# Quarter sums of the expert weights: loaded quarters against units already in SBUF

## The chip, the cores and the metric

The kernel runs on one core of a Trainium2 chip. The metric is the device time of one execution in microseconds (us). Engines are called as in the profile: PE (TensorE), PEld (its weight loads), DVE (VectorE), ACT (ScalarE), POOL (GpSimd) and SP (SyncE, which issues all of this kernel's DMAs).

## The reference

Attention over 8 batches of 12 heads, 448 positions, 64 elements a head, with a mix of the heads before and after the softmax; then an expert layer over all 3584 positions:

```
scores = einsum('bhij,hg->bgij', q @ k^T / 8, w_pre)
attn   = softmax(scores) ; attn = einsum('bhij,hg->bgij', attn, w_post)
x      = (attn @ v), heads side by side               # 3584 x 768
out    = ((x @ w1) * (x @ w2)) @ w3 @ w_out           # 768 -> 1024 -> 1024 -> 768
```

All in float32. The weights w1, w2, w3 and w_out come as float64.

## The kernel before

**The main loop.** `run` goes through N = 360 steps, 45 for each batch; a step handles 10 of the 448 rows of all 12 heads (120 partitions). The order of the work is written out by hand; each engine works through its own queue in that order. In step n stand, one behind the other: the fetch of the score rows of step n + 4 (L194), then whatever was put off to "later" (stores, loads of weights; `do_later`), splits of q and k for a later batch, the softmax of step n (DVE's reduce L218, ACT's exponent L221), the scaled mix weights of step n - 1 (L230 to L233), the split of the rows of step n + 2 into a rounded and a rest part (DVE L201, POOL L202), products q k^T of the next batch (L174, L175, left through ACT's copy L179 "st"), the work on expert weights that this text is about, half of the step's share of expert matmuls, the mix after the softmax for step n - 2 (`post`, L241, left through ACT's copy L247 "mt" out of bank 4), the products with v (L272), the other half of the expert matmuls, and the mix before the softmax for step n + 1 (L209 to L211). At the end `do_ends` issues the copies out of PSUM.

**Precision.** Products are made of float32 numbers split into a rounded part (type float32r) and a rest: three matmuls for each product (`PAIRS`). So a 128 x 128 block of a weight is kept as "hi" and "lo" side by side.

**The experts, batches 0 and 1 (`ONE` = 2).** `expert_atoms` makes the plain product, as background work of so many matmuls a step (`shares` spreads them evenly). The weights come in "units": for w1 and w2 one column block f of 128 with all six row blocks (768 KB, 18 matmuls), for the product w3 w_out, which is made beforehand, half a column block d (four row blocks, 512 KB, 12 matmuls). `next_unit` takes the next one, three buffers in pool "wp", two loads ahead. Batch 0's units of w1 and w2 are converted from float64 in SBUF and stored; all others are loaded (L354). Batch 0's first layer (288 matmuls) goes over steps 53 to 106, its output layer (144) and all of batch 1 (432) over steps 107 to 188, some 7 a step.

**The experts, batches 2 to 7.** From step 190 (`PAIR`) two batches at a time are multiplied by a scheme of seven products for 2 x 2 blocks in place of eight. Each weight is a 2 x 2 of quarters x11, x12, x21, x22, and four of the seven products need sums of quarters: number 7 is x11 - x21, number 5 is x21 + x22, number 6 is number 5 - x11, number 3 is x12 - number 6. These are stored split as "s_d" (L439) before step 190 and loaded by the pair stage.

**How the sums are made.** `combining` (L407 to L470) is a generator that is taken one piece further in each step once the conversion of units is over (L886). It has 12 sets: four for w1, four for w2, four for the third weight. A set takes 7 steps: two quarters are loaded (L423, tile "l", in the "s" buffers), in the next step DVE adds hi and lo of both (L430) and takes the first difference (L442); ACT and POOL split the result into an "s" tile (L436, L437), which is stored a step later (L439); then the other quarters are loaded in the same way, one a step. The "s" buffers are three, shared by the loads and the splits.

```
l11, l21 = (load(*sets[0], 0, i) for i in range(2))
yield
for i, (w, f) in enumerate(sets):
    x11, x21 = whole("x", f"x11{n}", l11), whole("x", f"x21{n}", l21)
    ...
    sum(s3, x11, x21, ALU.subtract)
    yield
```

Of the kernel before, what the change touches and what calls it, by code (L numbers as in the profile page):

```python
# [16 lines left out]
IB = 10  # L17
# [24 lines left out]
class Kernel:  # L42
# [219 lines left out]
    def av(self, b, a, g):  # L262
        nc, cols = self.nc, self.cols(a)
        W = cols.stop - cols.start
        if g % 3 == 0:
            self.i_psa = self.next_bank() if self.xq else 5
            self.psa = self.bank(self.i_psa, f"psa{b}_{a}_{g}")[:, :3 * GB * IB].rearrange("p (g i) -> p g i", g=3)
        v, mt = self.vs.pop((b, a, g)), self.mt[b, a]
        for j in range(NJ):
            for s in range(2):  # L270
                rows = slice(s * D, (s + 1) * D)
                nc.tensor.matmul(self.psa[rows, g % 3, :W], v[:, j, rows], mt[:, j, 2 * g + s, :W],  # L272
                                 start=(j == 0), stop=(j == NJ - 1))
        if g % 3 == 2 and b >= ONE:
            q, dst = self.psa[:, :, :W], self.x_d[b][g // 3][:, :, cols]
            x = self.staging(f"xd{b}_{a}_{g}")[:, :, :W]

            def leave():
                nc.scalar.copy(x, q)
                self.later.append(store)  # L280

            def store():
                nc.sync.dma_start(dst, x)
                self.x_made[b] += 1

            self.ends.append((self.i_psa, leave))
        elif g % 3 == 2:
            if b not in self.xs:
                pool = self.xp[b % 2]
                self.xs[b] = [pool.tile([128, K1, S], F32R, tag=f"x{t}", name=f"x{t}{b}") for t in "hl"]  # L290
            h, l = (x[:, g - 2:g + 1, cols] for x in self.xs[b])
            q = self.psa[:, :, :W]
            self.ends.append((5, lambda: nc.scalar.copy(h, q)))
            self.soon.append((5, lambda: nc.vector.tensor_tensor(l, q, h.bitcast(F32), op=ALU.subtract)))
        self.later.append(self.load_v)

    def staging(self, name):

        self.n_staging += 1
        if self.xq:  # L300
            return self.xq.tile([128, 3, GB * IB], F32, tag="x", name=name)
        t = self.xp[0].tile([128, K1, S], F32R, tag="xh" if self.n_staging % 2 else "xl", name=name)
        return t.bitcast(F32).rearrange("p k s -> p (k s)")[:, :3 * GB * IB].rearrange("p (k s) -> p k s", k=3)
# [44 lines left out]
    def units(self):  # L348
        return [u for b in range(ONE) for u in
                [(w, f, 0) for f in range(KF) for w in range(2)] + [(3, d, q) for d in range(K1) for q in range(2)]]  # L350

    def load_unit(self):
        t, src = self.unit_from(f"wu{self.n_loaded}", *self.unit_list[self.n_loaded])
        self.nc.sync.dma_start(t.bitcast(F32), src)  # L354
        self.loaded.append(t)
        self.n_loaded += 1
        self.n_asked -= 1

    def unit_of_one(self, name, w, f, q):
        t = self.wp.tile([128, K1, 2, 128], F32R, tag="w", name=name)  # L360
        if w < 2:
            return t, self.w_d[w][f]
        h = KF // 2
        return t[:, :h], self.w34_d[f][:, q * h:(q + 1) * h]

    def unit_of_pair(self, name, w, f, m):
        h, c = (K1 // 2, KF // 2) if w < 2 else (KF // 2, K1 // 2)
        t = self.wp.tile([128, KF // 2, 2, 128], F32R, tag="w", name=name)[:, :h]
        src = self.w_d[w] if w < 2 else self.w34_d
        if m in (1, 2, 4):  # L370
            return t, src[f + c * (m == 4)][:, h * (m > 1):h * (1 + (m > 1))]
        return t, self.s_d[w][m][f]
# [34 lines left out]
    def combining(self):  # L407

        nc, h = self.nc, K1 // 2
        sets = [(w, f) for w, f in [(0, 0), (1, 0), (0, 1), (1, 1), (0, 2), (1, 2), (0, 3), (1, 3)]]  # L410
        sets += [(2, f) for f in range(KF // 2)]

        def tile(name):
            return self.cs.tile([128, CW, 2], I32, tag="s", name=name, bufs=3).rearrange(
                "p n b -> p (n b)").bitcast(F32).rearrange("p (k t c) -> p k t c", k=h, t=2)

        def load(w, f, kh, fh):
            t = tile(f"l{w}_{f}_{kh}{fh}")
            if w < 2:
                src = self.w_d[w][f + fh * KF // 2][:, kh * h:(kh + 1) * h]  # L420
            else:
                src = self.w34_d[fh * h:(fh + 1) * h, :, f + kh * KF // 2].rearrange("d p t c -> p d t c")
            nc.sync.dma_start(t, src)  # L423
            return t

        def whole(tag, name, t):
            x = self.cs.tile([128, CW], F32, tag=tag, name=name, **({"bufs": 1} if tag == "m" else {}))
            x = x.rearrange("p (k c) -> p k c", k=h)
            if t is not None:
                nc.vector.tensor_tensor(x, t[:, :, 0], t[:, :, 1], op=ALU.add)  # L430
            return x

        def split(w, f, m, x):
            t = tile(f"s{w}_{f}_{m}")
            hi, lo = (t[:, :, i].bitcast(F32R) for i in range(2))
            nc.scalar.copy(hi, x)  # L436
            nc.gpsimd.tensor_tensor(lo, x, hi.bitcast(F32), op=ALU.subtract)  # L437
            dst = self.s_d[w][m][f] if w < 2 else self.s_d[w][m][:, :, f].rearrange("d p t c -> p d t c")
            self.later.append(lambda: nc.sync.dma_start(dst, t))  # L439

        def sum(out, x, y, op):
            nc.vector.tensor_tensor(out, x, y, op=op)  # L442

        l11, l21 = (load(*sets[0], 0, i) for i in range(2))
        yield
        for i, (w, f) in enumerate(sets):
            n = f"{w}_{f}"
            x11, x21 = whole("x", f"x11{n}", l11), whole("x", f"x21{n}", l21)
            s3 = whole("m", f"s3{n}", None)
            sum(s3, x11, x21, ALU.subtract)  # L450
            yield
            split(w, f, 7, s3)
            l22 = load(w, f, 1, 1)
            yield
            l12 = load(w, f, 1, 0)
            yield
            x22 = whole("m", f"x22{n}", l22)
            sum(x21, x21, x22, ALU.add)
            sum(x11, x21, x11, ALU.subtract)
            yield  # L460
            split(w, f, 5, x21)
            split(w, f, 6, x11)
            x12 = whole("m", f"x12{n}", l12)
            sum(x12, x12, x11, ALU.subtract)
            yield
            split(w, f, 3, x12)
            yield
            if i + 1 < len(sets):
                l11, l21 = (load(*sets[i + 1], 0, j) for j in range(2))
            yield  # L470
# [5 lines left out]
    def expert_atoms(self, b):  # L476
        nc, xs, hs = self.nc, self.xs.pop(b), []
        for f in range(KF):
            for i in range(2):
                w = self.next_unit()  # L480
                p = self.bank(6 + i, f"eg{b}_{f}_{i}")[:, :S]
# [18 lines left out]
            hs.append((h, l))  # L500
        self.do_ends()
        self.do_soon()
        for d in range(K1):
            p = self.bank(6 + d % 2, f"eo{b}_{d}")[:, :S]
            for k in range(KF):
                if k % (KF // 2) == 0:
                    w = self.next_unit()
                for t, (x, y) in enumerate(PAIRS):
# [6 lines left out]
            def leave(d=d, o=o, p=p, dst=dst):  # L515
                (nc.scalar.copy if d % 2 else nc.vector.tensor_copy)(o, p)
                self.later.append(lambda: nc.sync.dma_start(dst, o))

            self.ends.append((6 + d % 2, leave))
# [171 lines left out]
    def run(self):  # L691
# [5 lines left out]
        self.xq, self.n_staging = None, 0  # L697
# [5 lines left out]
        self.s_d = [{m: dp.tile([c, 128, k, 2, 128], F32, name=f"s{i}_{m}_d") for m in (3, 5, 6, 7)}  # L703
# [108 lines left out]
        self.unit_from, self.w_made, combining = self.unit_of_one, 2 * KF, self.combining()  # L812
        unit_pieces = self.converting(self.unit_jobs())
        nq, n_pieces = 0, -2
        for n in range(N + 6):
            if n == GB + 1:
                self.close("qp")
                self.xp = [self.pool("xp0", 1)]
            if n == SWITCH:
# [11 lines left out]
                background, total, done = self.experts(), (E_1 + E_2) * ONE, 0  # L831
            if n == PAIR:
                assert done == total and unit_pieces is None
# [4 lines left out]
                for _ in combining or ():  # L838
                    assert False
                self.close("sp", "hp", "xp1", "wp", "cs", "xp0")  # L840
                self.xq = self.pool("xq", 2)
# [44 lines left out]
            elif unit_pieces is None and combining and next(combining, self) is self:  # L886
                combining = None
# [78 lines left out]
```

## Time and profile before

| | us |
|---|---|
| median of 3 runs | 1742.28 (1741.29 to 1751.07) |
| profiled execution | 1747.12 |
| its span, first to last instruction | 1745.3 |
| mean granted PE clock | 0.967 |

| engine | busy us | share of the span |
|---|---|---|
| PE | 1616.8 | 93% |
| PEld | 1445.2 | 83% |
| DVE | 1110.5 | 64% |
| ACT | 929.9 | 53% |
| POOL | 1067.7 | 61% |

465 MB are moved in all, 266 GB/s over the span. Line numbers (L430) are those of the kernel before. In views of groups, "x48" is the number of instructions, followed by busy us, mean ns of one, and the idle time of the engine just before them with what ended it. In views of waits "A <- B: 82.6, 29, 8.4" says that A's engine sat idle 82.6 us in 29 places, at most 8.4 us, until B was done. In views of stretches each row begins with the stretch in us from the span's start; step 104 begins at 468 us, step 190 at 870 us.

### The profile page before, as it was taken

To read this page: it belongs to the slowest core of one execution; us is meant where nothing else is said; L and a number is where in the kernel's file an instruction comes from. 1 tells how busy PE (TensorE), PEld (TensorE's weight loads), DVE (VectorE), ACT (ScalarE), POOL (GpSimd) and SP (SyncE) were. 2 spreads that over 40 slices of the span, in tenths; PEclk is the share of its full clock that TensorE was granted. 3 is DMA by queue.
4 is the path that set the end of the run, shared out by engine and by line. 5 is a ranking of instruction groups with operands and counts; after the bars stand their busy time and mean duration, and the time that the engine had idled before them with its cause. 6 is when DMAs were issued, how large, how long until landed. Compare 5 with 4: busy or idle time off the path is not lost. (4 is left out here: it accounts for less than half of the span.)

```text
span 1745.3 us, 31764 instructions
## 1 busy us (share of the span) xinstructions
PE 1616.8 (93%) x10548; PEld 1445.2 (83%) x10548; DVE 1110.5 (64%) x2594; ACT 929.9 (53%) x2164; POOL 1067.7 (61%) x926
## 2 busy tenths in 40 slices
PE   4899998999989989888979999999999999999999
PEld 1479997887878878777869989989999899899988
DVE  4958657777656457556637557676665676844663
ACT  3867656767655455444545565556565444443222
POOL 2656545666655556455647677787676656756674
PEclk6999999999989999989989999999999999999999
DMA  7989778989889989988987898878987966669875
GB/s 257 289 261 286 242 214 259 290 282 305 265 275 326 339 289 313 327 261 274 309 271 231 267 298 241 264 243 259 334 271 243 265 188 196 196 212 321 279 233 183
DMA packets 242689, 464.97 MB, mean 266 GB/s; under 512 B 21854, under 2 KB 170590, under 8 KB 242526
## 3 DMA queue, kind: packets, MB, share of 16 engines
q1 hardware_dynamic: 242526, 462.95, 84.2%
q8 instruction: 84, 1.38, 0.3%
q14 instruction: 79, 0.65, 0.1%
HBM read 328.78 MB, written 134.09 MB: 265 GB/s over the span
## 5 line engine op out<-in xcount | busy, mean ns | idle before, releaser
L202 POOL TENSOR_TENSOR rl<-r,rh 120x448 fp32r<-120x448 f32 x360 | 430.3, 1196 | 487.3 <-DVE rh L201 136.7
L221 ACT ACTIVATE e<-psm,mn 120x448 f32<-120x448 f32 x360 | 228.6, 635 | 493.6 <-DVE sa L230 402.3
L241 PEld LDWEIGHTS pso<-w,e 120*112 120x112 f32 (+1 forms) x2880 | 354.9, 182 | 109.3 <-ACT mt L247 96.2
L218 DVE TENSOR_REDUCE mn<-psm 120x1 f32<-120x448 f32 x360 | 223.4, 621 | 344.7 <-PE psm L211 344.2
L241 PE MATMUL pso<-w,e 120*112 120x120 f32 (+1 forms) x2880 | 372.2, 274 | 70.0 <-ACT mt L247 69.7
L652 PE MATMUL e<-eh,wu 128*128 128x448 f32 x1008 | 305.7, 373 | 0.6 <-DVE c L606 0.5
L247 ACT COPY mt<-pso 112x480 f32<-112x480 f32 x360 | 206.2, 573 | 41.9 <-PE pso L241 41.0
L652 PEld LDWEIGHTS e<-eh,wu 128*128 128x128 f32 x1008 | 188.1, 189 | 15.7 <-DVE c L606 1.5
L201 DVE CAST rh<-r 120x448 fp32r<-120x448 f32 x360 | 184.6, 513 | 15.1 <-DMA r<-raw_d 14.6
L652 PE MATMUL e<-el,wu 128*128 128x448 f32 x504 | 187.7, 373 | 3.0 <-POOL el L591 3.0
L179 ACT COPY st<-psq 112x448 f32<-112x448 f32 x336 | 173.9, 528 | 28.9 <-DMA raw_d<-st 28.8
L233 DVE TENSOR_SCALAR w<-wpo,ri 120x120 f32<-120x120 f32 x360 | 161.8, 449 | 12.6
L209 PE MATMUL psm<-rh,wph 120*120 120x448 f32 x360 | 142.2, 395 | 20.0 <-DVE rh L201 20.0
L272 PE MATMUL psa<-mt,v 112*64 112x150 f32 (+1 forms) x2304 | 160.0, 296 | 0.0
L272 PEld LDWEIGHTS psa<-mt,v 112*64 112x64 f32 x2304 | 146.3, 139 | 6.6 <-issue 1.1
L484 PE MATMUL eg<-xh,wu 128*128 128x448 f32 x384 | 132.3, 395 | 7.3 <-ACT wu L113 4.5
L211 PE MATMUL psm<-rl,wph 120*120 120x448 f32 x360 | 134.9, 375 | 1.6 <-POOL rl L202 1.5
L164 POOL TENSOR_TENSOR ql<-kq,qh 128x448 fp32r<-128x448 f32 x84 | 97.5, 1160 | 61.1 <-ACT qh L162 60.8
L210 PE MATMUL psm<-rh,wpl 120*120 120x448 f32 x360 | 134.2, 373 | 0.0
L606 DVE TENSOR_TENSOR c<-c,e 128x448 f32<-128x448 f32 x168 | 100.9, 614 | 51.9 <-PE e L652 47.4
L174 PE MATMUL psq<-kk,qh 128*112 128x448 f32 x336 | 126.7, 377 | 6.7 <-ACT st L179 6.5
L175 PE MATMUL psq<-kk,ql 128*112 128x448 f32 x336 | 124.8, 371 | 0.0
(113 smaller groups left out, 2893.0 us busy)
## 6 DMA issues: line engine op xcount, KB each, us to landing
r<-raw_d SPq DMA_DIRECT2D x352, 210.0 KB, 4.0
raw_d<-st SPq DMA_DIRECT2D x168, 392.0 KB, 4.6
wu<-s_d SPq DMA_DIRECT2D x96, 384.0 KB, 4.2
v<-v SPq DMA_DIRECT2D x144, 224.0 KB, 4.8
kq<-kq SPq DMA_DIRECT2D x42, 672.0 KB, 7.4
wu<-w_d SPq DMA_DIRECT2D x72, 384.0 KB, 5.5
wu<-w_d SPq DMA_DIRECT2D x51, 512.0 KB, 6.1
l<-w_d SPq DMA_DIRECT2D x48, 384.0 KB, 7.3
```

Of the source, the lines that this page charges most:

```text
L179: copy(st[:, c % 2], p)
L201: nc.vector.tensor_copy(rh[:K], r[:K])
L202: nc.gpsimd.tensor_tensor(rl[:K], r[:K], rh[:K].bitcast(F32), op=ALU.subtract)
L209: nc.tensor.matmul(p[:K, :S], self.wph[:K, :K], rh[:K], start=True, stop=False)
L211: nc.tensor.matmul(p[:K, :S], self.wph[:K, :K], rl[:K], start=False, stop=True)
L218: nc.vector.tensor_reduce(mn[:K], p[:K, :S], axis=AX.X, op=ALU.min)
L221: nc.scalar.activation(e[:K], p[:K, :S], AF.Exp, bias=mn[:K], scale=-1.0, accum_out=sm[:K])
L233: nc.vector.tensor_scalar_mul(w2[:K, :, :w], wv[:K, :, :w], ri[:K])
L241: nc.tensor.matmul(p[:, j, :, :w], e[:K, j * JT:(j + 1) * JT], w2[:K, :, :w], start=True, stop=True)
L247: self.ends.append((4, lambda: copy(dst, p[:, :, :, :w])))
L272: nc.tensor.matmul(self.psa[rows, g % 3, :W], v[:, j, rows], mt[:, j, 2 * g + s, :W], start=(j == 0), stop=(j == NJ - 1))
L652: nc.tensor.matmul(p, w[:, k, x], ops[m, k][y], start=(k == 0 and t == 0), stop=(k == nk - 1 and t == 2))
```

## The change

`combining` and its 48 loads of quarters are gone. Where the experts take a unit whose quarters are wanted (the output layer of batch 0, the first layer of batch 1), `seen` is called: one step later DVE adds hi and lo straight from the unit's tile into a tile "y"; when both row halves of a block are there, `sums` takes the four sums in place over the next two steps, and the splits follow four to six steps after the unit was taken. `order` takes the blocks in the order 0, 4, 1, 5, ... (0, 3, 1, 4, ... for the output layer), so that the two blocks of a set are near each other. "y" has four buffers in a new pool "cb", made at step 107 together with the pool "xq" of the staged x, where the pool of batch 0's x is closed. A sum is stored with all hi ahead of all lo; for the third weight hi and lo are two stores, and lo is written over the sum in "y".

```
 def units(self):
     return [u for b in range(ONE) for u in
-            [(w, f, 0) for f in range(KF) for w in range(2)] + [(3, d, q) for d in range(K1) for q in range(2)]]
+            [(w, f, 0) for f in self.order(KF, b == 1) for w in range(2)] +
+            [(3, d, q) for d in self.order(K1, b == 0) for q in range(2)]]
...
+def seen(self, w, f, q, t):
+    c, k = (KF // 2, K1 // 2) if w < 2 else (K1 // 2, KF // 2)
+    halves = range(2) if w < 2 else (q,)
+    def whole():
+        if halves[0] == 0:
+            self.ys[w, f] = self.cb.tile([128, 2, 512], F32, tag="y", name=f"y{w}_{f}")
+        y = self.ys[w, f]
+        for i in halves:
+            u = t[:, i * k:(i + 1) * k] if w < 2 else t
+            u = u.bitcast(F32)
+            x = y[:, i, :k * 128].rearrange("p (k c) -> p k c", k=k)
+            self.nc.vector.tensor_tensor(x, u[:, :, 0], u[:, :, 1], op=ALU.add)
+    self.at(1, whole)
+    if f >= c and halves[-1] == 1:
+        self.sums(w, f - c, k)
+
+def sums(self, w, f, k):
+    ...
+    def first():
+        a, b = self.ys.pop((w, f)), self.ys.pop((w, f + c))
+        x.update({11: a[:, 0, :n], 12: a[:, 1, :n], 21: b[:, 0, :n], 22: b[:, 1, :n]})
+        nc.vector.tensor_tensor(x[11], x[11], x[21], op=ALU.subtract)
+        nc.vector.tensor_tensor(x[21], x[21], x[22], op=ALU.add)
+    def second():
+        nc.vector.tensor_tensor(x[22], x[22], x[11], op=ALU.subtract)
+        nc.vector.tensor_tensor(x[12], x[12], x[22], op=ALU.subtract)
+    def split(m, q):
+        s = self.cs.tile([128, CW, 2], I32, tag="s", name=f"s{w}_{f}_{m}", bufs=3)
+        ...
+        hi, lo = s[:, :n], s[:, n:2 * n] if w < 2 else x[q]
+        nc.scalar.copy(hi.bitcast(F32R), x[q])
+        nc.gpsimd.tensor_tensor(lo.bitcast(F32R), x[q], hi, op=ALU.subtract)
+        if w < 2:
+            self.later.append(lambda: nc.sync.dma_start(self.s_d[w][m][f], s))
         else:
+            self.later.append(lambda: nc.sync.dma_start(dst[:, 0], hi))
+            self.later.append(lambda: nc.sync.dma_start(dst[:, 1], lo))
+    self.at(2, first)
+    self.at(3, second)
+    for delay, m, q in ((4, 7, 11), (4, 5, 21), (5, 6, 22), (6, 3, 12)):
+        self.at(delay, lambda m=m, q=q: split(m, q))
...
 (expert_atoms)
+        for f in self.order(KF, b == 1):
             for i in range(2):
                 w = self.next_unit()
+                if b == 1:
+                    self.seen(i, f, 0, w)
...
+        if n == LATE:
+            self.close("xp0")
+            self.xq, self.cb = self.pool("xq", 2), self.pool("cb", 4)
...
-        elif unit_pieces is None and combining and next(combining, self) is self:
-            combining = None
+        self.do_timed()
```

More of the change, by code (lines that the diff above doesn't have):

```diff
@@ L265, in av @@
         if g % 3 == 0:
-            self.i_psa = self.next_bank() if self.xq else 5
+            self.i_psa = self.next_bank() if self.pairs else 5
             self.psa = self.bank(self.i_psa, f"psa{b}_{a}_{g}")[:, :3 * GB * IB].rearrange("p (g i) -> p g i", g=3)
@@ L275, in av @@
             q, dst = self.psa[:, :, :W], self.x_d[b][g // 3][:, :, cols]
-            x = self.staging(f"xd{b}_{a}_{g}")[:, :, :W]
+            x = self.xq.tile([128, 3, GB * IB], F32, tag="x", name=f"xd{b}_{a}_{g}")[:, :, :W]
             def leave():
@@ L295, in av @@
         self.later.append(self.load_v)
[L297 to L303, printed above, removed]
     def fold_jobs(self):
@@ L349, in units, with order @@
         return [u for b in range(ONE) for u in
-                [(w, f, 0) for f in range(KF) for w in range(2)] + [(3, d, q) for d in range(K1) for q in range(2)]]
+                [(w, f, 0) for f in self.order(KF, b == 1) for w in range(2)] +
+                [(3, d, q) for d in self.order(K1, b == 0) for q in range(2)]]
+    def order(self, n, summed):
+        return [i + j for i in range(n // 2) for j in (0, n // 2)] if summed else range(n)
     def load_unit(self):
-        t, src = self.unit_from(f"wu{self.n_loaded}", *self.unit_list[self.n_loaded])
+        t, view, src = self.unit_from(f"wu{self.n_loaded}", *self.unit_list[self.n_loaded])
         self.nc.sync.dma_start(t.bitcast(F32), src)
-        self.loaded.append(t)
+        self.loaded.append(view)
         self.n_loaded += 1
@@ L359, in unit_of_one @@
     def unit_of_one(self, name, w, f, q):
-        t = self.wp.tile([128, K1, 2, 128], F32R, tag="w", name=name)
+        t, h = self.wp.tile([128, K1, 2, 128], F32R, tag="w", name=name), KF // 2
         if w < 2:
-            return t, self.w_d[w][f]
-        h = KF // 2
-        return t[:, :h], self.w34_d[f][:, q * h:(q + 1) * h]
+            return t, t, self.w_d[w][f]
+        return t[:, :h], t[:, :h], self.w34_d[f][:, q * h:(q + 1) * h]
     def unit_of_pair(self, name, w, f, m):
         h, c = (K1 // 2, KF // 2) if w < 2 else (KF // 2, K1 // 2)
-        t = self.wp.tile([128, KF // 2, 2, 128], F32R, tag="w", name=name)[:, :h]
+        t = self.wp.tile([128, KF // 2 * 256], F32R, tag="w", name=name)[:, :h * 256]
         src = self.w_d[w] if w < 2 else self.w34_d
         if m in (1, 2, 4):
-            return t, src[f + c * (m == 4)][:, h * (m > 1):h * (1 + (m > 1))]
-        return t, self.s_d[w][m][f]
+            t = t.rearrange("p (k t c) -> p k t c", k=h, t=2)
+            return t, t, src[f + c * (m == 4)][:, h * (m > 1):h * (1 + (m > 1))]
+        return t, t.rearrange("p (t k c) -> p k t c", k=h, t=2), self.s_d[w][m][f]
     def unit_jobs(self):
@@ L403, in next_unit, with at @@
         return t
[L407 to L418, printed above, removed]
+    def at(self, delay, f):
+        self.timed.append((self.step + delay, f))
@@ new lines, in do_timed @@
+    def do_timed(self):
+        now = [f for n, f in self.timed if n <= self.step]
+        self.timed = [x for x in self.timed if x[0] > self.step]
+        for f in now:
+            f()
+    def seen(self, w, f, q, t):
[13 more added lines that the diff above has]
+            self.sums(w, f - c, k)
@@ new lines, in sums @@
+    def sums(self, w, f, k):
+        nc, c, n = self.nc, (KF // 2 if w < 2 else K1 // 2), k * 128
+        x = {}
+        def first():
[8 more added lines that the diff above has]
+            s = self.cs.tile([128, CW, 2], I32, tag="s", name=f"s{w}_{f}_{m}", bufs=3)
+            s = s.rearrange("p n b -> p (n b)").bitcast(F32)
+            dst = self.s_d[w][m][f].rearrange("p (t n) -> p t n", t=2)
+            hi, lo = s[:, :n], s[:, n:2 * n] if w < 2 else x[q]
+            nc.scalar.copy(hi.bitcast(F32R), x[q])
+            nc.gpsimd.tensor_tensor(lo.bitcast(F32R), x[q], hi, op=ALU.subtract)
@@ L419, in load @@
             if w < 2:
-                src = self.w_d[w][f + fh * KF // 2][:, kh * h:(kh + 1) * h]
+                self.later.append(lambda: nc.sync.dma_start(self.s_d[w][m][f], s))
             else:
[L422 to L470, printed above, removed]
+                self.later.append(lambda: nc.sync.dma_start(dst[:, 0], hi))
@@ L476, in expert_atoms @@
     def expert_atoms(self, b):
-        nc, xs, hs = self.nc, self.xs.pop(b), []
-        for f in range(KF):
+        nc, xs, hs = self.nc, self.xs.pop(b), {}
+        for f in self.order(KF, b == 1):
             for i in range(2):
                 w = self.next_unit()
+                if b == 1:
+                    self.seen(i, f, 0, w)
                 p = self.bank(6 + i, f"eg{b}_{f}_{i}")[:, :S]
@@ L499, in expert_atoms @@
             self.soon.append((None, parts))
-            hs.append((h, l))
+            hs[f] = h, l
         self.do_ends()
         self.do_soon()
-        for d in range(K1):
-            p = self.bank(6 + d % 2, f"eo{b}_{d}")[:, :S]
+        for n, d in enumerate(self.order(K1, b == 0)):
+            p = self.bank(6 + n % 2, f"eo{b}_{d}")[:, :S]
             for k in range(KF):
@@ L507, in expert_atoms @@
                     w = self.next_unit()
+                    if b == 0:
+                        self.seen(2, d, k // (KF // 2), w)
                 for t, (x, y) in enumerate(PAIRS):
@@ L513, in expert_atoms, with leave @@
             dst = self.out[d * 128:(d + 1) * 128, b * S:(b + 1) * S]
-            def leave(d=d, o=o, p=p, dst=dst):
-                (nc.scalar.copy if d % 2 else nc.vector.tensor_copy)(o, p)
+            def leave(n=n, o=o, p=p, dst=dst):
+                (nc.scalar.copy if n % 2 else nc.vector.tensor_copy)(o, p)
                 self.later.append(lambda: nc.sync.dma_start(dst, o))
-            self.ends.append((6 + d % 2, leave))
+            self.ends.append((6 + n % 2, leave))
     def pair_units(self):
@@ L696, in run @@
         self.slot, self.free, self.keep, self.x_made, self.n_groups = {}, list(range(NS)), [], [0] * B, 0
-        self.xq, self.n_staging = None, 0
+        self.timed, self.ys, self.pairs = [], {}, False
         dp = self.pool("dram", 1, space=DRAM)
@@ L702, in run @@
         self.x_d = [dp.tile([2, 128, K1 // 2, S], F32, name=f"x{b}_d") for b in range(B)]
-        self.s_d = [{m: dp.tile([c, 128, k, 2, 128], F32, name=f"s{i}_{m}_d") for m in (3, 5, 6, 7)}
+        self.s_d = [{m: dp.tile([c, 128, k * 256], F32, name=f"s{i}_{m}_d") for m in (3, 5, 6, 7)}
                     for i, (c, k) in enumerate(((KF // 2, K1 // 2), (KF // 2, K1 // 2), (K1 // 2, KF // 2)))]
@@ L811, in run @@
         self.unit_list, self.loaded, self.n_loaded, self.n_asked, self.w_ahead = self.units(), [], 0, 0, 2
[L812 removed]
+        self.unit_from, self.w_made = self.unit_of_one, 2 * KF
         unit_pieces = self.converting(self.unit_jobs())
@@ L815, in run @@
         for n in range(N + 6):
+            self.step = n
             if n == GB + 1:
@@ L831, in run @@
                 background, total, done = self.experts(), (E_1 + E_2) * ONE, 0
+            if n == LATE:
+                assert done >= E_1
+                self.close("xp0")
+                self.xq, self.cb = self.pool("xq", 2), self.pool("cb", 4)
             if n == PAIR:
-                assert done == total and unit_pieces is None
+                assert done == total and unit_pieces is None and not self.timed
                 next(background, None)
@@ L837, in run @@
                 self.do_later()
[L838 to L841, printed above, removed]
+                self.pairs = True
+                self.close("sp", "hp", "xp1", "wp", "cs", "cb")
                 self.wp = self.pool("wp", 5, side="right")
```

## The prediction

> **What bounds the kernel now.** I read the page first, then busy time by stage, then the waits of DVE and PE in the one stage that the change touches, then the instructions around one of those waits in order of time. A "step" is one turn of the main loop; each has one softmax reduce (L218), so counting L218 in a stretch counts its steps. The three long stretches below are most of batch 0's first layer (305.5 to 456.1), the stage in which the sums are made now (466 to 870) and a part of the pair stage (918.2 to 1290). Columns: length, busy us and instruction count of each engine (PE, PEld, DVE, ACT, POOL), granted clock, DMA share, GB/s.
>
> ```profile
> 305.50:456.10 150.60, 141.29 (x1013) 123.82 (x1013) 117.49 (x308) 106.22 (x251) 101.56 (x91) 1.00 0.92 288
> 466.00:870.00 404.00, 351.23 (x2312) 315.43 (x2310) 236.90 (x543) 202.81 (x484) 219.91 (x192) 0.93 0.93 301
> 918.20:1290.00 371.80, 368.48 (x2536) 338.35 (x2535) 249.50 (x571) 220.06 (x510) 267.06 (x226) 1.00 0.86 270
> 550.00:600.00 50.00, 45.79 (x312) 41.70 (x312) 28.96 (x66) 26.37 (x63) 27.53 (x25) 0.90 0.98 326
> 1600.00:1700.00 100.00, 99.25 (x489) 91.08 (x488) 63.47 (x83) 25.40 (x50) 70.45 (x59) 1.00 0.82 258
> ```
>
> The same three stretches for L218 alone (DVE's count is that of the steps), and for the experts' matmuls alone (PE and PEld; L484 in two stretches, then L509, then L652):
>
> ```profile
> 305.50:456.10 150.60, 24.77 (x40) 1.00 0.92 288
> 466.00:870.00 404.00, 53.35 (x87) 0.93 0.93 301
> 918.20:1290.00 371.80, 55.93 (x90) 1.00 0.86 270
> ```
>
> ```profile
> 305.50:456.10 150.60, 55.60 (x204) 35.66 (x204) 1.00 0.92 288
> 466.00:870.00 404.00, 83.31 (x310) 58.26 (x310) 0.93 0.93 301
> ```
>
> ```profile
> 466.00:870.00 404.00, 76.34 (x288) 53.31 (x288) 0.93 0.93 301
> ```
>
> ```profile
> 918.20:1290.00 371.80, 190.07 (x776) 139.84 (x776) 1.00 0.86 270
> ```
>
> In the pair stage PE idles 1% and a step takes 371.8 / 90 = 4.13 us with 776 / 90 = 8.6 expert matmuls; PE sets it. In the tail, where PE does nothing else, 489 of them take 100 us: 0.204 us each. The sums' stage has (310 + 288) / 86 = 6.95 expert matmuls a step (the 87th reduce only starts there), and PE's other work per step is that of the pair stage, so PE alone would need 4.13 - 1.67 x 0.204 = 3.79 us. It takes 404 / 86 = 4.70. So **78 us** (86 x 0.91) of this stage are not PE's work at full clock. They show as 53 us of idle PE and a clock of 0.93 instead of 1.00, some 28 us. By the same working batch 0's first layer needs 3.41 us and takes 3.77: 0.35 us a step too long at a DMA share of 0.92, with the clock at 1.00.
>
> What ends the idle times (who <- releaser: us, times, longest), DVE's and PE's in 466 to 870, then DVE's and PE's in 305.5 to 456.1:
>
> ```profile
> DVE x L430 <- DMA l<-w_d: 82.6, 29, 8.4
> DVE mn L218 <- PE psm L211: 75.0, 39, 6.1
> ```
>
> ```profile
> PE pso L241 <- ACT mt L247: 44.2, 14, 6.5
> PE psq L174 <- ACT st L179: 3.8, 1, 3.8
> PE eg L484 <- DVE em L491: 2.4, 1, 2.4
> PE eo L509 <- DMA wu<-w_d: 2.2, 1, 2.2
> ```
>
> ```profile
> DVE mn L218 <- PE psm L211: 24.7, 14, 3.1
> ```
>
> ```profile
> PE pso L241 <- ACT mt L247: 9.1, 13, 1.5
> ```
>
> DVE waits 82.6 us for the quarters that the sums load; in the stretch before it waits for PE and hardly else. One such wait in order of time:
>
> ```profile
> 505.59 2.72 SPq L423 DMA_DIRECT2D l<-w_d  x2
> ...
> 513.52 0.56 DVE L430 TENSOR_TENSOR x<-l 128x384 f32<-128x384 f32 x1 [5.79 <-DMA l<-w_d]
> ...
> 516.39 0.63 ACT L221 ACTIVATE e<-psm,mn 120x448 f32<-120x448 f32 x1 [7.54 <-DVE sa L230]
> ...
> 517.59 0.72 PE L174 MATMUL psq<-kk,qh 128*112 128x448 f32 x1 [3.83 <-ACT st L179]
> ...
> 522.09 0.37 PE L174 MATMUL psq<-kk,qh 128*112 128x448 f32 x1
> ```
>
> Two loads are issued at 505.6; DVE has stood at the first add for 5.8 us when it can run. The softmax reduce queued behind it is late, so ACT's exponent and, behind that in ACT's queue, the copies that free PE's banks; PE runs dry for 3.8 us, and its next matmul takes 0.72 us where the same one takes 0.37 us a step later. Twelve sets, each with such a wait, make the 78 us.
>
> The half rate after 3.8 us of idling is what the 0.93 is made of. The Trainium skill, TensorE: Matmul & The Clock Gate (Part 1), says that PE drops to half clock after an idle window of about 3.4 us and is back after as long a busy one; the 0.72 against 0.37 agrees. By that rule the clock's 28 us come back whole once no wait is that long; if the clock followed PE's mean load instead, half might stay away and the time below would be 14 us longer.
>
> **The change part by part.** *Removed: 48 loads* of 384 KB, and with them DVE's wait. Rows of 466 to 870: the DMA issues (count, KB each, median us to landing), and the sums' operations (busy, mean ns):
>
> ```profile
> l<-w_d SPq DMA_DIRECT2D x48, 384.0 KB, 7.3
> s_d<-s SPq DMA_DIRECT2D x48, 384.0 KB, 4.7
> ```
>
> ```profile
> L442 DVE TENSOR_TENSOR x<-x,x 128x384 f32<-128x384 f32 x36 | 40.1, 1114 | 1.2
> L437 POOL TENSOR_TENSOR s<-x,s 128x384 fp32r<-128x384 f32 x36 | 39.1, 1098 | 0.0
> L430 DVE TENSOR_TENSOR x<-l 128x384 f32<-128x384 f32 x48 | 30.6, 638 | 82.6 <-DMA l<-w_d 82.6
> L436 ACT CAST s<-x 128x384 fp32r<-128x384 f32 x36 | 17.5, 523 | 0.0
> ...
> L437 POOL TENSOR_TENSOR s<-s,s 128x384 fp32r<-128x384 f32 x12 | 12.0, 999 | 0.0
> L442 DVE TENSOR_TENSOR s<-x,x 128x384 f32<-128x384 f32 x12 | 6.7, 558 | 1.2
> L436 ACT CAST s<-s 128x384 fp32r<-128x384 f32 x12 | 6.3, 521 | 0.0
> ```
>
> The bytes are 48 x 393216 = 18.9 MB; at 301 / 0.93 = 324 GB/s they took 58 us of the 16 DMA engines, out of 0.93 x 404 = 376. If everything they cost went, the gain would be the 78 us.
>
> *Kept, moved together.* The adds are the same elements in other cuts (32 of 384 and 12 of 512 where there were 48 of 384), so are the sums and splits: DVE 77 us (40.1 + 30.6 + 6.7), POOL 51, ACT 24. Now they follow the units: output layer of batch 0 (144 matmuls) and first layer of batch 1 (288), at 7 a step from step 108. By the planned shares the first add stands in step 109, the first split in 117, the last in 171. So DVE's work falls in 63 steps and the splits and stores in 54, instead of 86. DVE's rest is (237 - 77) / 86 = 1.86 us a step, plus 77 / 63 = 1.22: 3.1 of some 4.1. POOL 1.96 + 51 / 54 = 2.9, ACT 2.08 + 0.44 = 2.5. None becomes the bound; I cost this at nothing, under PE's 3.79.
>
> *The stores crowd.* Without loads and stores the DMA engines have (376 - 116) / 86 = 3.02 us of work a step; with the stores' 58 us over 54 steps 4.10. At the best share quoted, 0.98, that is 4.18 us, more than PE's 3.79. So in those 54 steps DMA sets the pace: 54 x 4.18 = 226. The other 32 steps at 3.79 and 0.1 for bumps: 124. Together 350, a gain of **54 us**. Taking batch 0's excess of 0.35 for all steps instead gives 86 x 4.14 = 356, a gain of 48.
>
> *New waits.* An add stands in the step after its unit was first multiplied, when it has landed. But ACT's copy needs one of three "s" buffers, held until its store lands: copy 0.52, POOL 1.1, landing 4.7, and some 1.3 of SP's turn, 7.6 us. Counting the steps of the splits, 17 of the 44 reuse a buffer two steps later (8 us: near nothing, up to 0.6 each by the spread of landings) and 4 one step later (where the sets of both weights meet, at steps 139 and 169: 4 x 3.6 = 14 us). Behind ACT's copy stand the bank copies, so PE would see it. Bounds: 0, if a step's slack covers it, and 25 x 0.94 = 24 us at the rate at which DVE's wait cost PE (78 / 82.6). I take **7**, the two long meetings half covered, since 13 small waits of PE before step 104 left the clock at 1.00. A DVE add may also wait for one of four "y" buffers whose store is out; three places by the steps, 1 to 4 us each, 0 to 10 in all, taken as 0. The unit's buffer is held by the add no longer than by its matmuls.
>
> *At nothing:* the output layer's other order, the buffers made at step 107, the other layout inside a stored sum (128 adjacent columns either way), the two halves stored apart for the third weight (8 issues more on SP, against 48 fewer). The pair stage's start finds the stores done earlier; DVE waits there (870 to 1060) for rows, which a quieter DMA could help: 0 to 14.6, taken as 0.
>
> ```profile
> DVE rh L201 <- DMA r<-raw_d: 14.6, 4, 6.1
> ```
>
> **Sum:** 54 - 7 = 47 us, 2.7%. On the profiled execution 1747.1 - 47 = 1700; the median shown is 4.8 lower, so **1695**.
>
> **The rivals.**
> 1. *PE alone is left, 1666.* DMA gives more than 326 GB/s when asked, and PE gets its 3.79: the whole 78, less 2. For it: 326 GB/s is what was moved, not a limit seen. Against: the share of 0.98 there. The Trainium skill, HBM Reference (Specifications), puts a core streaming alone at about 425 GB/s; no stretch quoted here comes near it. By that figure this rival would be the forecast.
> 2. *Waits in new places, 1719.* The "s" waits cost their upper end, 24, and DMA's lateness batch 0's 0.35 a step, 30: 78 - 54 leaves 23. For it: 44 splits in 54 steps on three buffers. Against: ACT idles half the time (404 - 203).
> 3. *The change only renames the wait, 1741.* If the units land as late as the quarters did, 28 of them with 2 us each cost 56, and the adds hold DVE as before: 54 - 56. For it: units of 768 KB are twice a quarter's size. Against: PE needs the unit a step earlier, and waits 2.2 us for units in all (L509's row above).
> 4. *Slower, 1761.* ACT's wait at the splits runs away: with landings slower in the crowd a buffer comes back after 12 us instead of 7.6; then the 17 two-step reuses wait 4 each and the 4 one-step ones 8: 100 us, at 0.94 a loss of 94 against 76. It outweighs the gain from about 11 us on. Against: 4.10 us of DMA work a step is below the 376 / 86 = 4.37 of now.
>
> **How the numbers follow.** Forecast 0.58 (own range 1676 to 1712), rival 1: 0.13, rival 2: 0.18, rival 3: 0.07, rival 4: 0.04. The range 1664 to 1728 takes in rivals 1 and 2 and leaves out 3, 4 and some tails, under 0.2. 1% is 17.4 us, about what a measurement can tell from no change: faster means below 1724.9. That holds for the forecast, for rival 1 and two thirds of rival 2, less some tails: 0.82; slower 0.05; the rest 0.13.
>
> **What would show it.** Right: no wait of DVE for a load at the adds; 86 steps in some 357 us; clock at 0.98 or more there; a DMA share of 0.95 or more while the stores go and about 0.8 afterwards; PE idle under 20 us. Wrong: ACT's copy waiting for the store of "s" and PE for "mt"; DVE waiting at the adds; the clock still at 0.93; any change of pace after 918 us, where the same work is left.

## The result, and the profile after

| | before | after |
|---|---|---|
| median, us | 1743.53 of 4 runs (1741.29 to 1751.07) | 1702.11 of 4 runs (1701.03 to 1705.28) |
| profiled execution, us | 1747.12 | 1705.28 |
| its span, us | 1745.3 | 1703.5 |
| mean granted PE clock | 0.967 | 0.974 |

The ratio is 0.9758, with a 95% interval of 0.9725 to 0.9791: 2.4% faster, 41.4 us in medians. The forecast was 47 us and a time of 1695.

Nearly all of it lies in the stage of the sums. Steps 104 to 190 took 402.3 us (467.6 to 869.9) and now take 360.9 (469.7 to 830.7). Of these, steps 117 to 171, in which the sums are split and stored, go at 4.44 us a step, the 13 ahead of them at 3.76 and the 19 behind them at 3.82. From step 190 on the pace stays as it was: the rest takes 872.8 us, and took 875.5.

Busy time by stretch of the kernel after; the columns are those of the prediction (length, PE, PEld, DVE, ACT, POOL, clock, DMA share, GB/s). The first row is the whole stage, the second the steps ahead of the splits, the third the steps with splits, the fourth those after them, and the last some ten steps out of the third:

```profile
470.00:831.00 361.00, 335.10 (x2301) 303.40 (x2299) 247.09 (x534) 203.11 (x476) 228.21 (x187) 0.97 0.87 283
470.00:519.00 49.00, 49.00 (x357) 45.20 (x356) 30.14 (x77) 27.64 (x64) 26.75 (x22) 1.00 0.87 266
519.00:758.00 239.00, 215.56 (x1467) 194.19 (x1466) 184.35 (x359) 134.49 (x317) 165.66 (x133) 0.96 0.90 298
761.00:831.00 70.00, 67.54 (x463) 61.18 (x462) 30.85 (x94) 38.11 (x89) 33.36 (x31) 1.00 0.78 246
...
572.00:611.00 39.00, 36.69 (x241) 31.84 (x240) 36.68 (x69) 22.68 (x54) 27.11 (x22) 1.00 0.92 312
```

PE's idle time in the stage fell from 53 us to 26, nearly all of it (23) in the third row, and the clock came back from 0.93 to 0.97. But look at the third row's other columns: the DMA share is 0.90, not full, while DVE is busy 184 of 239 us, and in the last row 36.7 of 39, as much as PE.

What ends DVE's idle times in 470 to 831, then ACT's, then PE's (who <- releaser: us, times, longest), in the kernel after:

```profile
DVE mn L218 <- PE psm L211: 100.6, 48, 10.5
DVE rh L201 <- POOL kk L165: 2.3, 1, 2.3
DVE rh L201 <- DMA r<-raw_d: 1.7, 1, 1.7
DVE y L427 <- DMA s_d<-y: 1.1, 1, 1.1
```

```profile
ACT e L221 <- DVE sa L230: 90.3, 58, 4.5
ACT s L453 <- DMA s_d<-s: 19.7, 7, 4.5
```

```profile
PE pso L241 <- ACT mt L247: 20.0, 8, 5.8
```

DVE's 82.6 us for loaded quarters are gone; the add itself (now L427) waits 1.1 us in one place. In their place ACT waits 19.7 us for the stores that hold the "s" buffers (L453 is its half of the split), and PE waits 20.0 us (44.2 before) for the bank copy that ACT makes (L247).

The same kernel in order of time, where the sets of two weights meet (steps 139 to 141):

```profile
611.43 0.93 ACT L453 CAST s<-y 128x384 fp32r<-128x384 f32 x2
...
614.57 2.62 SPq L456 DMA_DIRECT2D s_d<-s  x3
614.93 0.51 ACT L453 CAST s<-y 128x384 fp32r<-128x384 f32 x1 [2.57 <-DMA s_d<-s]
615.35 0.56 ACT L247 COPY mt<-pso 112x480 f32<-112x480 f32 x1
...
615.96 1.94 PE L241 MATMUL pso<-w,e 120*112 120x120 f32 x8 [5.11 <-ACT mt L247]
...
621.44 0.51 ACT L453 CAST s<-y 128x384 fp32r<-128x384 f32 x1 [4.49 <-DMA s_d<-s]
```

Two splits have used up the buffers, the third stands 2.57 us until a store has landed, the bank copy queued behind it follows at once, and PE has been idle for 5.11 us when it can go on. Its eight matmuls then take 1.94 us (eight of the same line take 0.98 in the next fence but one), so this wait also costs clock. The fourth split waits again, 4.49 us. The other meeting, at 749.6 and 754.1 (ACT's work of steps 169 and 170), has the same form with waits of 4.02 and 2.51 us.

DVE's instructions for the sums in the kernel after, by form (count, busy us, mean ns of one, idle time ahead):

```profile
L427 DVE TENSOR_TENSOR y<-wu 128x384 f32<-128x384 f32 x32 | 35.9, 1162 | 1.1 <-DMA s_d<-y 1.1
L446 DVE TENSOR_TENSOR y<-y,y 128x384 f32<-128x384 f32 x8 | 11.1, 1390 | 0.3
L442 DVE TENSOR_TENSOR y<-y 128x384 f32<-128x384 f32 x8 | 11.1, 1390 | 0.3
L427 DVE TENSOR_TENSOR y<-wu 128x512 f32<-128x512 f32 x12 | 10.1, 840 | 0.0
L445 DVE TENSOR_TENSOR y<-y,y 128x384 f32<-128x384 f32 x8 | 6.3, 786 | 0.0
L441 DVE TENSOR_TENSOR y<-y,y 128x384 f32<-128x384 f32 x8 | 5.4, 671 | 0.0
```

Four more groups of three instructions each, with 512 elements, make 13.4 us more: 93 in all. The 44 adds cost 46.0 us where 48 cost 30.6, though they add the same elements; the differences cost what they did (47.3 us against 46.8). So the adds became slower, from 638 ns to 1162 for the same 384 elements. One step of the kernel after shows how:

```profile
596.56 0.55 DVE L445 TENSOR_TENSOR y<-y,y 128x384 f32<-128x384 f32 x1
...
596.77 1.35 POOL L202 TENSOR_TENSOR rl<-r,rh 120x448 fp32r<-120x448 f32 x1 [1.96 <-issue]
...
597.14 1.39 DVE L446 TENSOR_TENSOR y<-y,y 128x384 f32<-128x384 f32 x1
...
597.61 0.98 PE L241 MATMUL pso<-w,e 120*112 120x120 f32 x8
...
598.07 1.46 POOL L164 TENSOR_TENSOR ql<-kq,qh 128x448 fp32r<-128x448 f32 x1
...
598.46 1.49 DVE L427 TENSOR_TENSOR y<-wu 128x384 f32<-128x384 f32 x1
```

DVE's operation that starts before POOL's subtraction takes 0.55 us; one of the same size that starts beside it takes 1.39 and ends 0.41 us after POOL does, nearly as if it had begun only when POOL was done; the next, beside POOL's next subtraction, takes 1.49 and ends 0.42 us after it. The Trainium skill, SBUF — State Buffer (SBUF: two separate sides), describes this: a DVE operation with two SBUF inputs and a GpSimd operation that reads SBUF take turns on one pair of ports, each for the whole instruction. The rows agree. Before, 41 of the 48 adds began while POOL had nothing running and took about 0.55 us (in the stretch that the prediction quotes, 0.56 at 513.5); 7 began beside a POOL operation and took 1.12 on average. Now 24 of the 44 begin beside one and take 1.46.

The wait that was taken away had kept adds and POOL apart, but its loss is only part of the excess: with the old adds and the wait alone gone (the first experiment) the mean rises from 638 ns to 830, 8.4 of the 15.4 us. No run tells what the rest is; the trace points to the new places of the adds, for 15 of the 24 are the second of two adds in a row, which begins beside a POOL operation whether or not the first did.

### The profile page after: what moved, and what is told of

Its sections match the earlier page's. It is cut to its first block, busy times and chain, and to the rows that moved or that the text cites. A ratio compares the mean times of both kernels' runs of the same rounds, so it can differ in the third digit from the quotient of the medians.

```text
span 1703.5 us, 31656 instructions
## 1 busy us (share of the span) xinstructions
PE 1601.2 (94%) x10548; PEld 1433.5 (84%) x10548; DVE 1122.4 (66%) x2586; ACT 932.3 (55%) x2160; POOL 1078.5 (63%) x922
## 5 line engine op out<-in xcount | busy, mean ns | idle before, releaser
L202 POOL TENSOR_TENSOR rl<-r,rh 120x448 fp32r<-120x448 f32 x360 | 436.8, 1213 | 438.2 <-DVE rh L201 146.4
L241 PEld LDWEIGHTS pso<-w,e 120*112 120x112 f32 (+1 forms) x2880 | 350.4, 179 | 80.4 <-ACT mt L247 66.5
L241 PE MATMUL pso<-w,e 120*112 120x120 f32 (+1 forms) x2880 | 366.4, 271 | 43.8 <-ACT mt L247 43.7
L247 ACT COPY mt<-pso 112x480 f32<-112x480 f32 x360 | 206.4, 573 | 38.5 <-PE pso L241 37.8
L201 DVE CAST rh<-r 120x448 fp32r<-120x448 f32 x360 | 177.0, 492 | 21.1 <-DMA r<-raw_d 18.2
```

What stands on the lines that cost most here:

```text
L201: nc.vector.tensor_copy(rh[:K], r[:K])
L202: nc.gpsimd.tensor_tensor(rl[:K], r[:K], rh[:K].bitcast(F32), op=ALU.subtract)
L241: nc.tensor.matmul(p[:, j, :, :w], e[:K, j * JT:(j + 1) * JT], w2[:K, :, :w], start=True, stop=True)
L247: self.ends.append((4, lambda: copy(dst, p[:, :, :, :w])))
```

## The experiments

Two questions. What of the change brought the 41 us: the end of DVE's wait, or 18.9 MB less to move? And what holds steps 117 to 171 at 4.44 us: the DMA engines (the forecast), ACT's wait for the "s" buffers, or DVE's longer queue?

**The wait alone.** The kernel before with its 48 loads kept, but issued five or six steps ahead of the add, into four buffers of their own ("lp"):

```
+        def early(name):
+            return self.lp.tile([128, CW, 2], I32, tag=name[-2:], name=name)...
         def load(w, f, kh, fh):
-            t = tile(f"l{w}_{f}_{kh}{fh}")
+            t = (early if self.lp else tile)(f"l{w}_{f}_{kh}{fh}")
...
             yield
-            l12 = load(w, f, 1, 0)
+            if i + 1 < len(sets):
+                l11, l21 = (load(*sets[i + 1], 0, j) for j in range(2))
```

> The kernel before with all its 48 loads of quarters, but each issued five or six steps ahead of its add, in four buffers of their own (from the second set on). Theory 'the wait': the 78 us came from DVE standing at the add, so they go although the bytes stay: DVE's wait for l falls from 82.6 us to under 10, the stage from 404 to 345-365 us, the time to 1690-1708. Rival 'the bytes': the 58 us that the DMA engines spend on these loads are what counts; 376 us of DMA work at a share of 0.98 need 384 us, so the time is 1722 or more.

Measured: 1707.43 us, ratio 0.9796 (0.9767 to 0.9825): 36 of the 41 us, with every byte still moved, at the upper end of what was expected of the wait and below the 1722 of the bytes. (Its interval overlaps that of the kernel after, so the other 5 us are not clear of noise.) Its stretches (the stage, then 526 to 754, which are steps 117 to 171), DVE's wait for the loads, the adds by form, and the loads' landing in its DMA issues:

```profile
468.00:831.00 363.00, 335.87 (x2298) 302.90 (x2297) 241.59 (x541) 202.66 (x478) 220.90 (x190) 0.97 0.99 333
526.00:754.00 228.00, 212.07 (x1468) 191.13 (x1467) 152.25 (x339) 128.44 (x303) 141.00 (x121) 0.98 1.00 339
```

```profile
DVE x L434 <- DMA l<-w_d: 4.9, 2, 4.4
```

```profile
L434 DVE TENSOR_TENSOR x<-l 128x384 f32<-128x384 f32 x48 | 39.0, 830 | 4.9 <-DMA l<-w_d 4.9
```

```profile
l<-w_d SPq DMA_DIRECT2D x48, 384.0 KB, 7.6
```

A load still takes 7.6 us, but it now lands before DVE asks for it: 4.9 us of waiting are left of 82.6. So the wait is what the change took away. The DMA columns show the next limit: 1.00 busy at 339 GB/s. The loads fit here, but only just.

**The bytes alone.** The kernel after with 48 loads of 384 KB that nobody reads, one in each of steps 109 to 156:

```
+            if LATE + 2 <= n < LATE + 50:
+                self.extra_load(n - LATE - 2)
```

> The changed kernel plus 48 loads of 384 KB (half of them in two pieces), one a step in steps 109 to 156, into buffers that nobody reads. 'The wait': within 6 us of the changed kernel, 1700-1708, since DMA was busy 0.87 of the stage only. 'The bytes': its 314 us of DMA work grow to 372, which at 0.98 take 380 us instead of 361: 1720 or more.

Measured: 1726.92 us, ratio 0.9898 (0.9877 to 0.9919), 25 us above the kernel after. The theory of the wait alone had them within 6 us, so it missed; that of the bytes had 1720 or more. Stretch 516 to 778 is steps 117 to 171 of this kernel; then ACT's waits:

```profile
516.00:778.00 262.00, 220.17 (x1470) 197.20 (x1469) 179.65 (x360) 135.34 (x316) 163.93 (x133) 0.94 1.00 335
```

```profile
ACT s L453 <- DMA s_d<-s: 33.5, 14, 5.1
ACT st L179 <- DMA raw_d<-st: 17.6, 9, 4.5
```

The DMA engines are full for all of it. The kernel after moves 298 x 239 = 71.2 MB in these steps; the 40 loads that fall into them make it 86.9 MB, which at the 339 GB/s of the run above take 256 of the 262 us. The stores land late (those of 384 KB take 6.4 us in these steps, 4.6 in the kernel after), and ACT waits for their buffers. With loads and stores spread over 86 steps the bytes cost at most the 5 us between the run above and the kernel after; with the stores in 54 steps and the loads in 48 of nearly the same ones they cost 25. So the bytes do count once the stores are crowded. The extra loads also lengthen SP's queue: in these steps SP stood some 12 us until their own buffers were free. How much of the 25 us that is was not told apart.

**ACT's buffers.** The kernel after with a fourth "s" buffer:

```
         def split(m, q):
-            s = self.cs.tile([128, CW, 2], I32, tag="s", name=f"s{w}_{f}_{m}", bufs=3)
+            self.n_split += 1
+            pool, bufs = (self.cs, 3) if self.n_split % 4 < 3 else (self.cs2, 1)
+            s = pool.tile([128, CW, 2], I32, tag="s", name=f"s{w}_{f}_{m}", bufs=bufs)
```

> The changed kernel with four s buffers instead of three, so that no split reuses a buffer one step later. Theory 'ACT's buffer wait': ACT's 19.8 us of waiting for the store of s fall under 5, PE's waits of 5.1 and 5.8 us for mt in steps 140 and 170 go, with the half clock behind them: 14 to 20 us, 1682-1689. Rival 'DVE is full': DVE, idle 2 us in 41 in steps 130 to 139, holds the softmax anyway, and only some 5 us come: 1695-1699. Rival 'DMA's pace' of 4.18 us a step from the prediction: at most 3 us, 1699 or more.

Measured: 1694.77 us (1693.11 to 1700.59), ratio 0.972 (0.9696 to 0.9744): 7 us below the kernel after. No run of one lies among those of the other, though the intervals of the two ratios overlap. The stage, ACT's wait and PE's:

```profile
466.00:819.00 353.00, 333.01 (x2302) 302.11 (x2300) 246.18 (x534) 202.89 (x475) 228.08 (x186) 0.98 0.90 290
```

```profile
ACT s L455 <- DMA s_d<-s: 2.1, 2, 1.4
```

```profile
PE pso L241 <- ACT mt L247: 12.5, 7, 3.2
```

ACT's 19.7 us shrank to 2.1, the stage by 8 us. The theory that ACT's buffers hold the stage expected 14 to 20 us, so half or more of that something else still holds; a full DVE, the rival, had 1695 to 1699.

**DVE's sums.** That kernel without its 44 differences (the adds, splits and stores remain):

```
         def first():
             ...
-            nc.vector.tensor_tensor(x[11], x[11], x[21], op=ALU.subtract)
-            nc.vector.tensor_tensor(x[21], x[21], x[22], op=ALU.add)
-        def second(): ...
...
-        self.at(3, second)
```

> As e3 with four s buffers, and DVE's 44 sums (differences and totals, 36 us of DVE) left out; splits and stores stay, so what is stored is not the sums. 'DVE is full': 8 to 15 us below e3, the waits of PE for mt in steps 149 to 161 gone. 'DMA's pace': within 3 us of e3, the stores being the same.

Measured: 1679.37 us, ratio 0.9625 (0.9605 to 0.9645), 15 us below the kernel with four buffers. The stage, and in the second row steps 117 to 171; then PE's wait:

```profile
467.00:807.00 340.00, 328.86 (x2303) 300.00 (x2303) 204.73 (x490) 203.17 (x475) 220.49 (x187) 0.99 0.92 302
516.00:732.00 216.00, 208.57 (x1471) 189.81 (x1470) 145.82 (x320) 135.22 (x317) 157.75 (x133) 0.99 0.96 322
```

```profile
PE pso L241 <- ACT mt L247: 3.1, 4, 1.5
```

The same bytes and stores now go in 216 / 54 = 4.0 us a step; at 4.18 DMA could not have let them. So the work of the differences, not DMA, held these steps: PE's wait for the bank copy falls from 12.5 to 3.1 us when DVE has less to do, for the copy stands behind ACT's exponent, and that behind DVE's reduce and L230. (POOL, beside which they ran, also became lighter, 228.1 to 220.5 us in the stage; that share was not told apart.) What the remaining 0.2 above PE's 3.79 is made of stays open; the DMA share of 0.96 suggests DMA.

**Relieving DVE, two ways.** First, with four buffers, the rounding of the score rows (L201) goes to ACT in steps 115 to 171; second, instead of that, 22 of the 44 differences go to POOL; third, both.

```
-        nc.vector.tensor_copy(rh[:K], r[:K])
+        (nc.scalar.copy if LATE + 8 <= n - 2 < LATE + 65 else nc.vector.tensor_copy)(rh[:K], r[:K])
```

> As e3 (four s buffers), and the rounding of the score rows (L201) on ACT instead of DVE in steps 115 to 171: some 0.45 us a step off DVE, 25 us in all, ACT then busy 0.66 of the stage. 'DVE is full': by e4's 15 us for 36 us of DVE, 7 to 11 us below e3, 1684-1688, and the waits of PE for mt in steps 149 to 161 under 1.5 us. Rival 'ACT is in the path': ACT now stands at the rows' load ahead of its other copies, and the gain is eaten: 1693 or more.

```
         def second():
-            nc.vector.tensor_tensor(x[22], x[22], x[11], op=ALU.subtract)
-            nc.vector.tensor_tensor(x[12], x[12], x[22], op=ALU.subtract)
+            nc.gpsimd.tensor_tensor(x[22], x[22], x[11], op=ALU.subtract)
+            nc.gpsimd.tensor_tensor(x[12], x[12], x[22], op=ALU.subtract)
```

> As e3, and two of each set's four sums (22 operations, some 23 us of DVE) on POOL. 'DVE is full': 6 to 10 us below e3, 1685-1689. Rival 'POOL paces the rows' (SP's fetches wait for POOL's split of the rows, 147 us in e3): what DVE gains POOL loses, 1693 or more.

> e5 and e6 together, some 48 us off DVE. 'DVE is full': as low as e4, where 36 us of DVE were left out, 1677-1683. Rival: ACT or POOL become what is late, not below the better of e5 and e6.

Measured: on ACT 1688.30 us, ratio 0.9684 (0.9662 to 0.9705); on POOL 1695.03, 0.9724 (0.9705 to 0.9742); both 1688.88, 0.9682 (0.9663 to 0.9701). The stage with the rounding on ACT, with its groups by form:

```profile
468.00:816.00 348.00, 331.91 (x2302) 301.03 (x2300) 204.19 (x476) 228.43 (x532) 222.05 (x186) 0.98 0.90 294
```

```profile
L201 ACT CAST rh<-r 120x448 fp32r<-120x448 f32 x56 | 31.3, 558 | 2.9 <-PE psm L210 2.1 <-DMA r<-raw_d 0.4 <-PE pso L241 0.4
...
L427 DVE TENSOR_TENSOR y<-wu 128x384 f32<-128x384 f32 x32 | 28.8, 941 | 2.7 <-DMA s_d<-y 2.7
```

The stage with the differences on POOL:

```profile
468.00:821.00 353.00, 333.47 (x2298) 301.08 (x2297) 244.86 (x510) 202.76 (x474) 249.67 (x208) 0.98 0.89 289
```

On ACT, 57 roundings of 0.56 us left DVE 42 us lighter (246.2 to 204.2) and the run 6 us shorter, just outside the 1684 to 1688 of a full DVE. DVE lost the roundings, and what it kept became faster: the differences took 34.6 us instead of 47.1, the adds of 384 elements 941 ns instead of 1132, though those of 512 went from 840 to 1110. On POOL, DVE lost 22 operations and 1.3 us: what was left of its work got slower beside POOL's longer queue (the roundings, L201, took 55.7 us instead of 44.5), and nothing was gained; the rival there had 1693 or more. Both together brought no more than ACT alone. These two versions, 13.8 and 13.2 us below the kernel after with intervals of the ratios that do not overlap with its own, are the fastest of those that make the sums.

Lightening DVE by as much as leaving the differences out does (204.7) brought 6 us rather than 15. That ACT's new load is the reason is not shown: with both moves DVE is lighter still (198.2), and PE waits no longer for ACT's bank copies than without the differences (3.1), yet the run is 9.5 us above that one. Its row (8.9 us with the rounding on ACT, 12.5 with four buffers alone):

```profile
PE pso L241 <- ACT mt L247: 3.2, 6, 1.1
```

Part of the gain is lost in the steps that follow. Steps 117 to 171 took 231.8 us with four buffers, 223.2 with the rounding on ACT, 220.8 with both moves and 216.3 without the differences. The 19 steps behind them took 72.2 us with four buffers and 76.3, 77.9 and 75.4 in the other three. In those three PE waits there once, for 3.7 to 4.8 us, until a unit of weights has landed (2.4 with four buffers), and the clock is 0.96 to 0.98 instead of 1.00. The two stretches of the run with both moves:

```profile
515.40:736.20 220.80, 210.59 (x1472) 189.49 (x1471) 138.52 (x285) 158.84 (x370) 180.27 (x155) 0.99 0.95 314
736.20:814.10 77.90, 72.67 (x482) 65.83 (x480) 32.28 (x98) 41.51 (x98) 36.61 (x32) 0.96 0.81 261
```

What else parts these runs from the one without the differences stays open.

**The order of units.** The kernel before, with only the order of column blocks of the change:

```
+    def order(self, n, summed):
+        return [i + j for i in range(n // 2) for j in (0, n // 2)] if summed else range(n)
```

> The kernel before with nothing but the other order of the units (0, 4, 1, 5, ... in batch 1's first layer, 0, 3, 1, 4, ... in batch 0's output layer). All theories: no difference, within 4 us of the kernel before, 1740-1748; if the order itself brought something, the sums' part would be smaller by as much.

Measured: 1744.5 us, ratio 1.0 (0.9986 to 1.0014). The order costs and gives nothing, and DVE's wait is as long as before:

```profile
DVE x L435 <- DMA l<-w_d: 82.1, 29, 9.4
```

## Why the prediction was right, and where not

- **What bounds the kernel: right.** DVE's wait for the quarters was the cause. Taken away with the bytes kept, it gave 36 of the 41 us.
- **The clock: right.** It rose to 0.97 in the stage (0.98 was said) and is 1.00 outside steps 117 to 171. What is missing stands behind the long waits that are left, as the slow eight matmuls at 616 show.
- **The steps without splits, 32 at 3.89: right.** 13 took 3.76 and 19 took 3.82 us, 121 us against 124. PE alone was estimated at 3.79.
- **The step that failed: "None becomes the bound; I cost this at nothing."** DVE's work for the sums was put at 77 us, with the adds at their old mean of 638 ns, when most of them began with POOL idle. It measured 93, nearly all of the excess in the adds, over half of which now begin beside a POOL operation. DVE is busy 184.35 / 54 = 3.4 us a step (3.1 was said) and for stretches as long as PE, and the reduce of the softmax, queued behind the sums, is late for ACT and PE. Leaving out the differences gave back 15 us.
- **"DMA sets the pace", 4.18 us a step: wrong in cause, near in size by luck.** The share is 0.90, not the 0.95 said. The 324 to 326 GB/s taken as the limit are not one (339 were moved with early loads); at that rate the 298 x 239 / 54 = 1.32 MB a step need 3.9 us. With the buffer wait gone the 54 steps took 4.29 us each, close to 4.18, but without the differences and with the same stores 4.0. A DMA cost put too high and a DVE cost left out nearly cancel.
- **The "s" buffers: right.** The two places named, steps 139 and 169, are where ACT's long waits begin; each goes on into the next step. The price was put at 7 us and measured 7 to 8 with a fourth buffer. The 14 us of ACT's waiting put on the two meetings were 7.1 and 6.5; the other 6.1 of ACT's 19.7 us stand elsewhere.
- **At nothing: right** for the order (measured by itself) and for the pair stage, whose pace did not change and whose wait for rows hardly did (16.5 us). The "y" buffers cost 1.1 us of DVE.
- **The signs.** There is no long wait at the adds, and the DMA share behind the splits is 0.78, as said. PE idles 26 us, not under 20. One of the signs of being wrong did show: ACT waits 19.7 us for the stores of "s" and PE 20.0 for "mt". It stood in the sum with 7 us.
- **The sum.** 54 steps at 4.31 with the buffer wait were said and 4.44 measured: 7 us. The other 32 steps gave back 3. That leaves 361 us against 357, and the stage before, counted by its steps, was 402.3 us and not the 404 of the stretch: 41.4 of gain for 47.
- **The rivals.** The first, PE alone, is 36 us below the measured time: the fourth buffer gave 7 of these, leaving out the differences 15, and 13 stay open. The second had the right place at ACT's buffers and an upper end, 24, of which 7 to 8 were there. The third, the wait renamed, is excluded by the 1.1 us at the adds. The fourth, slower, had the right place: ACT at the splits, but a buffer comes back in time. It took the extra loads to bring part of it about. Two of the rivals' sums are off, with nothing hanging on it: 78 - 54 is 24, not 23, and 54 - 56 gives 1744, not 1741.

## What to carry to other kernels

When one engine's wait for a transfer sets a stage, issuing the transfer earlier may give nearly all that removing it gives; whether the bytes matter is read from the DMA share of the steps into which the rest of the traffic then falls. A mean duration holds for the neighbours beside which it was measured, and a wait can have kept them idle: before using it in a sum, look whether the same operation also appears beside the other engine's work, and what it took there. Where DVE is crowded, try its one-input copies on ACT before its two-input operations on POOL: here the first brought 6 us and the second nothing.

## What the runs showed of the hardware

A DVE operation on two SBUF inputs of 384 elements takes about 0.55 us when it begins with POOL idle, and in the rows above 1.39 and 1.49 when it begins beside a POOL subtraction. The mean goes by how many do: 638 ns with 7 of 48 adds beside POOL, 830 with 14 of 48 (early loads), and 1162 in the kernel after, with 22 of its 32 adds of this size. Moving 22 differences to POOL took only 1.3 us off DVE's 246. The DMA engines moved 339 GB/s over 228 us at a share of 1.00 with the early loads, and 335 GB/s over 262 us at the same share with the unread ones.
